# Moving w_out, g and graw by 64 bytes modulo 256 in SBUF, relative to x and w_in

## The chip, the cores and the metric

The kernel runs on one core of a Trainium2 chip. Its time is the device time of one execution in microseconds, from which a median of three runs is taken. A profile belongs to one further execution, with its own time.

## What is computed

18 blocks of 256 tokens go through an attention within chunks of 64 tokens, and then through a feed-forward layer with a rational function between its two products:

```
scores = scale * q_c @ k_c^T;  attn = softmax(scores);  x = attn @ v_c      # per chunk of 64, per head
h = x @ w_in                                   # (4608, 512) @ (512, 2048)
P = a0 + a1*h + a2*h^2 + a3*h^3
Q = 1 + |b0|*|h| + |b1|*h^2
g = P / (Q + 1e-6)
out = g @ w_out                                # (4608, 2048) @ (2048, 512)
```

## The kernel before

Each of x, w_in, g and w_out is split into a high part (F32R, a copy that keeps the upper bits) and a low part (the rest), and a product is the sum of high by high, high by low and low by high. Four kinds of work stand on TensorE:

- **ff1** (`ff1`, L340 to L352): h of one step, that is 512 of the 2048 hidden columns of one block. A call makes two of four groups of 12 matmuls 128x128 by 128x256; the weights that are loaded come from `wi_hi` or `wi_lo`, the moving operand from `xhi` or `xlo`. The result goes to the PSUM tile `ph`. A step has 48 matmuls, mostly in one run.
- **Second product in the early part** (`ff2`, L407 to L431): 48 matmuls for a step. Here g is loaded as weights (`ghi`, `glo`) and `wo` moves. Each pair covers the 512 columns of `wo` in two pieces of 256; at two places the cut is moved: by `CUT_FIRST` (24 columns) behind the small attention matmuls, and by `CUT_LAST` (48 columns: 304 and then 208) where an ff1 run comes next.
- **Second product in the fast part** (`fast_raw`, `fast_sum`, L624 to L643, all recorded at L619): from the seventh block on, a step takes 42 matmuls by a scheme with seven products for eight. The weights come from `graw` (18 matmuls) and from `shi` and `slo` (24), which lie in the buffers tagged `ghi` and `glo`; `wo` moves. There is no shifted cut here.
- **Attention**: 64 small matmuls (`quarters`, L225) for scores and for values, 8 transposes (L304).

The order is written out by hand: `START` for the first six blocks, `STEADY` for every later block. In `STEADY` a block has four ff1 runs; behind each stands the second product of an earlier step, and in three of the four the attention matmuls of a later block stand inside it: values behind 18 matmuls, scores behind 12, transposes behind 18. So the uninterrupted runs of the second product are 18 and 24, 12 and 30, 42, and again 18 and 24.

VectorE, ScalarE and GpSimd compute the rational function between the two products. SyncE's queue refetches parts of `wo` from DRAM (`fetch`, L601 to L604), since the scheme needs sums of blocks of w_out that replace some of its columns.

**Where the tiles lie.** Tiles lie behind each other in each partition's row of SBUF in the order in which they are first made. Their start addresses modulo 256 bytes, in the program as built, are: `wi_hi` and `wi_lo` 128, `xhi` and `xlo` 64, `wo` 128, the `ghi` and `glo` buffers 64, `graw` 64 (its buffer starts at 192, and 96 unused columns of 4 bytes stand ahead of it: 192 + 384 = 576). The slices that one matmul reads start at multiples of 512 bytes behind these, but for the shifted cuts. So while a weight load runs beside the matmul ahead of it, their operands start 64 bytes apart in one direction within ff1 (weights 128, moving 64), 64 bytes apart in the other direction within the second product (weights 64, moving 128), and at the same place modulo 256 where the one kind follows the other: the first weights of g (64) beside the last x (64), and the first weights of w_in (128) beside the last `wo` (128).

Of the kernel before, what the change touches and what calls it, by code (L numbers as in the profile page):

```python
# [10 lines left out]
F32 = mybir.dt.float32  # L11
F32R = mybir.dt.float32r
# [6 lines left out]
P = 128  # L19
# [56 lines left out]
def tile_chunked_attention_rational_moe(  # L76
# [12 lines left out]
    cp = ctx.enter_context(tc.tile_pool(name="cp", bufs=1))  # L89
    p2 = ctx.enter_context(tc.tile_pool(name="p2", bufs=2))  # L90
# [6 lines left out]

    wi_hi = cp.tile([P, NHP, DFF], F32R, tag="wi_hi", name="wi_hi")
    wi_lo = cp.tile([P, NHP, DFF], F32R, tag="wi_lo", name="wi_lo")
    wo = cp.tile([P, 2, 16, DM], F32R, tag="wo", name="wo")  # L100
    wo_hi, wo_lo = wo[:, 0], wo[:, 1]
    ident = cp.tile([P, P], F32, tag="ident", name="ident")
# [235 lines left out]
    ch, gbuf, obuf, accs = {}, {}, {}, {}  # L338
# [46 lines left out]

    def chain_ghi(n, s):
        h, A, B, C = ch[n, s]
        gbuf[n, s] = [p2.tile([P, FPS, BT], F32R, tag="ghi", name=f"ghi{n}_{s}"), None]
        nc.vector.scalar_tensor_tensor(gbuf[n, s][0], C, a0, A, ALU.add, ALU.mult)  # L389

# [39 lines left out]
                )  # L430
        before[0] = "ff2"  # L431

    co = p2.tile([P, 128], F32, tag="co", name="co", bufs=1)
    na0, na1, na2, na3, c0, kq, lsc, ebias, ib, b1m, nib = (co[:, i:i + 1] for i in range(11))

    def newton_reciprocal(_):
# [15 lines left out]
    def fast(g):  # L452
        return NST * FAST <= g < total - 2

    sbuf, graw = {}, {}
# [44 lines left out]
    def quads(x):  # L500
        return x.rearrange("p (j k) (i t) -> p j (k i) t", k=2, i=2)

    def new_hr(g):
        key = steps[g]
        C = ch[key][3]
        if not fast(g):
            gbuf[key] = [p2.tile([P, FPS, BT], F32R, tag="ghi", name=f"ghi{g}"), None]
            nc.scalar.copy(gbuf[key][0], C)
            return
        if g % 2 not in graw:  # L510
            t = p2.tile([P, 96 + 1536], F32R, tag="raw", name=f"graw{g % 2}", bufs=3)
            graw[g % 2] = t[:, 96:].rearrange("p (h j q t) -> p h j q t", h=2, j=2, q=3)
        nc.scalar.copy(graw[g % 2][:, 0], quads(C)[:, :, 1:4, :])  # L513

    def new_lr(g):
# [278 lines left out]
    for letter, f in zip("abcQIJpPgHRG", (  # L794
        chain_a, chain_b, chain_c, chain_q, chain_ln, chain_exp,
        chain_p, chain_p2, chain_ghi, chain_r1, chain_r2, chain_glo,
    )):
        do[letter] = of_step(f)
    do["Gp"] = lambda g: chain_glo(*steps[g], nc.gpsimd)
    for name, f in (  # L800
        ("ua", new_u), ("uc", new_c), ("uQ", new_v), ("uI", new_ln), ("uJ", new_exp), ("up", new_p), ("uP", new_p2),
        ("ug", new_t), ("uH", new_inv), ("uR", new_g), ("ue", new_hr), ("uGp", new_ls),
        ("uG", lambda g: new_ls(g, nc.vector)),
    ):
        do[name] = f

    def run(program, then=""):
# [11 lines left out]
    chain = {  # L819
        "U": new_u, "C": new_c, "V": new_v, "p": new_p, "p2": new_p2, "Ln": new_ln, "Ex": new_exp, "t": new_t,  # L820
        "A2": new_inv, "g": new_g, "hR": new_hr, "lR": new_lr, "s1": new_s1, "s2": new_s2, "s4": new_s4,
        "hS": new_hs, "lS": new_ls,
    }
# [81 lines left out]
    for b in range(FAST, NB + 1):  # L905
# [5 lines left out]
        for op, stage, shift in order:  # L911
# [3 lines left out]
            if stage is not None:  # L915
                g = NST * n + int(stage)
# [45 lines left out]
```

## Time and profile before

| | us |
|---|---|
| median of three runs | 872.11 (872.03 to 872.94) |
| the profiled execution | 870.93 |
| its span, first to last instruction | 869.1 |
| TensorE busy | 835.3 (96%) |
| VectorE busy | 741.9 (85%) |
| ScalarE busy | 539.1 (62%) |
| GpSimd busy | 523.5 (60%) |

The profiled execution is 1.2 us under the median, and 1.8 us of it lie outside the span. Matmuls are pipelined, so a matmul's own duration (some 279 ns) says little; the distance from the start of one to the start of the next, its pitch, is what adds up. Counts in the view of stretches include the matmuls that reach over a stretch's borders, so for the number in a run the code's count is taken.

### The profile page before, as it was taken

The page shows a single profiled execution, that of the slowest core. Times are in us where ns is not written, and L with a number is a line of the kernel's source. Part 1 is how long each engine was busy: PE and PEld are TensorE (multiplying, and loading weights), DVE is VectorE, ACT ScalarE, POOL GpSimd, SP SyncE. Part 2 cuts the span into 40 slices and gives each one's busy share as a digit, 9 for nine tenths or more (in the row PEclk, how much of TensorE's full clock was granted, in tenths as well). Part 3 has the DMA queues.
Part 4 walks back from the last instruction along what each step waited for, and adds up shares of the span by engine and source line. Part 5 has one row for each costly group of instructions (what it writes and reads, how often), then busy time and mean ns, then how long its engine had stood idle before and what let it go on. Part 6 is the DMA issues. An engine that isn't in the chain of part 4 may idle for free.

```text
span 869.1 us, 20986 instructions
## 1 busy us (share of the span) xinstructions
PE 835.3 (96%) x9084; PEld 825.7 (95%) x9084; DVE 741.9 (85%) x644; ACT 539.1 (62%) x541; POOL 523.5 (60%) x325
## 2 busy tenths in 40 slices
PE   2799989999999999999999999999999999999997
PEld 2799989999999999999999999999999999999996
DVE  5999997888778887888888888888888888898785
ACT  5998856466474656565666566666665665565652
POOL 1223234602877096776777777777787767686761
PEclk9999999999999999999999999999999999999999
DMA  8644433103132355767777786767676867766761
GB/s 317 252 174 155 146 123 91 32 2 99 49 122 74 133 193 163 237 216 227 243 239 245 220 253 205 253 214 251 210 252 221 254 219 248 236 220 203 257 212 33
DMA packets 125468, 162.85 MB, mean 187 GB/s; under 512 B 6848, under 2 KB 111296, under 8 KB 122304
## 3 DMA queue, kind: packets, MB, share of 16 engines
q1 hardware_dynamic: 125216, 161.25, 56.8%
q8 instruction: 71, 1.16, 0.6%
q10 hardware_dynamic: 160, 0.26, 0.1%
q14 instruction: 21, 0.17, 0.1%
HBM read 142.61 MB, written 18.87 MB: 186 GB/s over the span
## 4 chain that ended last, share of the span: by engine, by line
PE 86%; DVE 6%; DMA 4%; ACT 2%; issue 2%; SPq 1%; DVEq 0%; ACTq 0%
PE ph L352 41%; PE acc L619 14%; PE po L428 13%; PE acd L619 11%; DMA wo<-t 2%; PE psx L225 2%; PE pss L225 2%; PE pst L304 2%; DVE B L368 1%; DMA Bqk<-in_kT 1%; DMA raw<-in_w_out 1%; DMA out<-o 1%; DVE raw L186 1%; DVE B L393 0%; DVE C L380 0%
## 5 line engine op out<-in xcount | busy, mean ns | idle before, releaser
L352 PE MATMUL ph<-xhi,wi_hi 128*128 128x256 f32 x1152 | 321.6, 279 | 0.2 <-ACT at L308 0.2
L352 PE MATMUL ph<-xlo,wi_hi 128*128 128x256 f32 x1152 | 320.2, 278 | 0.8 <-DVE xlo L335 0.8
L352 PE MATMUL ph<-xhi,wi_lo 128*128 128x256 f32 x1152 | 319.9, 278 | 0.0
L352 PEld LDWEIGHTS ph<-xhi,wi_hi 128*128 128x128 f32 x1152 | 217.3, 189 | 0.9 <-ACT at L308 0.4
L352 PEld LDWEIGHTS ph<-xlo,wi_hi 128*128 128x128 f32 x1152 | 216.5, 188 | 1.3 <-DVE xlo L335 1.3
L352 PEld LDWEIGHTS ph<-xhi,wi_lo 128*128 128x128 f32 x1152 | 216.6, 188 | 0.0
L460 ACT ACTIVATE U<-ph 128x1024 f32<-128x1024 f32 x57 | 58.6, 1029 | 156.5 <-PE ph L352 156.1
L550 POOL TENSOR_TENSOR slo<-B,shi 128x1024 fp32r<-128x1024 f32 x46 | 110.7, 2407 | 69.7 <-ACT shi L542 67.5
L469 DVE SCALAR_TENSOR_TENSOR U<-U,co 128x1024 f32<-128x1024 f32 x57 | 98.2, 1724 | 23.9 <-ACT U L460 22.7
L490 DVE SCALAR_TENSOR_TENSOR U<-U,co,ph 128x1024 f32<-128x1024 f32 x57 | 71.9, 1262 | 44.4 <-ACT ph L486 44.1
L526 POOL TENSOR_TENSOR B<-C 128x512 f32<-128x512 f32 x46 | 68.7, 1494 | 54.6 <-DVE C L498 49.1
L428 PE MATMUL po<-wo,ghi 128*128 128x256 f32 (+3 forms) x768 | 94.0, 279 | 0.0
L428 PEld LDWEIGHTS po<-wo,ghi 128*128 128x128 f32 x768 | 91.0, 189 | 0.4 <-DVE ghi L389 0.2
L518 POOL TENSOR_TENSOR graw<-C,graw 128x768 fp32r<-128x768 f32 x46 | 85.5, 1859 | 0.7 <-ACT graw L513 0.7
L482 ACT ACTIVATE B<-U,cst,co 128x1024 f32<-128x1024 f32 x57 | 70.8, 1245 | 17.2 <-DVE U L469 16.8
L619 PE MATMUL acc<-wo,graw 128*128 128x256 f32 x552 | 79.4, 279 | 0.0
L486 ACT ACTIVATE ph<-B,co 128x1024 f32<-128x1024 f32 x57 | 63.9, 1120 | 17.5 <-DVE C L477 17.3
L498 DVE SCALAR_TENSOR_TENSOR C<-C,co,ph 128x1024 f32<-128x1024 f32 x57 | 73.0, 1281 | 2.0
L477 DVE SCALAR_TENSOR_TENSOR C<-C,co,ph 128x1024 f32<-128x1024 f32 x57 | 72.8, 1277 | 1.4
L494 DVE SCALAR_TENSOR_TENSOR ph<-U,ph 128x1024 f32<-128x1024 f32 x57 | 69.9, 1226 | 1.5
L619 PEld LDWEIGHTS acc<-wo,graw 128*128 128x128 f32 x552 | 70.0, 188 | 0.7
L473 DVE TENSOR_TENSOR C<-C,ph 128x1024 f32<-128x1024 f32 x57 | 69.0, 1210 | 1.8 <-ACT C L465 1.7
(105 smaller groups left out, 1630.1 us busy)
## 6 DMA issues: line engine op xcount, KB each, us to landing
wo<-t SPq DMA_DIRECT2D x90, 768.0 KB, 6.7
wo<-t SPq DMA_DIRECT2D x98, 256.0 KB, 3.3
out<-o SPq DMA_DIRECT2D x68, 128.0 KB, 6.3
raw<-in_w_out SPq DMA_DIRECT2D x8, 1024.0 KB, 5.1
raw<-in_w_in SPq DMA_DIRECT2D x8, 1024.0 KB, 5.1
v<-in_vP SPq DMA_DIRECT2D x20, 256.0 KB, 7.4
qk<-in_qT SPq DMA_DIRECT2D x36, 128.0 KB, 6.8
qk<-in_kT SPq DMA_DIRECT2D x36, 128.0 KB, 6.6
```

The costliest lines, as they stand in the source:

```text
L352: nc.tensor.matmul(ph[:, fi, :], w[:, cc, f], x[:, cc, :], start=(k == 0), stop=(k == len(mm) - 1))
L428: nc.tensor.matmul(accs[n][i][:, cols], g[:, fi, i * 128:(i + 1) * 128], w[:, FPS * s + fi, cols], start=start, stop=stop,)
L469: nc.vector.scalar_tensor_tensor(U, U, c0, U, ALU.add, ALU.mult)
L473: nc.vector.tensor_mul(C, C, h)
L477: nc.vector.scalar_tensor_tensor(C, C, na1, h, ALU.add, ALU.mult)
L482: nc.scalar.activation(ch[key][2], ch[key][1], AF.Ln, bias=cst[:, 0:1], scale=lsc)
L490: nc.vector.scalar_tensor_tensor(V, V, kq, h, ALU.add, ALU.mult)
L494: nc.vector.scalar_tensor_tensor(h, V, 2.0, h, ALU.subtract, ALU.mult)
L498: nc.vector.scalar_tensor_tensor(C, C, na0, h, ALU.add, ALU.mult)
L518: nc.gpsimd.tensor_sub(lo, quads(ch[steps[g]][3])[:, :, 1:4, :], hi.bitcast(F32))
L550: nc.gpsimd.tensor_sub(lo, sbuf[g], hi.bitcast(F32))
L619: nc.tensor.matmul(acc[n][pair][:, bank, col:col + 256], stat, mov, start=start, stop=stop)
```

## The change

Three tiles get other padding. 16 columns of 4 bytes ahead of `wo` move it by 64 bytes; 16 columns ahead of the first `ghi` buffer move `ghi` and `glo`; the padding inside `graw`'s buffer becomes 48 columns. The tile `co`, of which 11 columns are used, shrinks from 128 to 48 columns, by 320 bytes, so that with the 64 ahead of `wo` all between moves by a multiple of 256. Every instruction stays where it was on its engine, with the same operands and shapes; only addresses differ.

After it the starts modulo 256 are: `wi` 128 and x 64 as before; `wo` 192; `ghi`, `glo` and `graw` 128. Within ff1 and within the second product the distances between weights and moving operand are the same as before. Where the one kind follows the other they are now those of the kind that ends: g's weights (128) beside the last x (64), as w_in's weights stood beside x; w_in's weights (128) beside the last `wo` (192), as g's stood beside `wo`. At a cut shifted by 48 columns the last piece of `wo` starts 192 bytes further, before at 64, now at 128. `ident`, `nident`, `ab` and `cst` move by 64 bytes too; the attention's and the chain's tiles keep their places modulo 256.

```diff
@@ -97,6 +97,7 @@
     wi_hi = cp.tile([P, NHP, DFF], F32R, tag="wi_hi", name="wi_hi")
     wi_lo = cp.tile([P, NHP, DFF], F32R, tag="wi_lo", name="wi_lo")
+    cp.tile([P, 16], F32, tag="gap", name="wo_gap")
     wo = cp.tile([P, 2, 16, DM], F32R, tag="wo", name="wo")
@@ -385,6 +386,8 @@
     def chain_ghi(n, s):
         h, A, B, C = ch[n, s]
+        if not gbuf:
+            p2.tile([P, 16], F32, tag="gap", name="gap", bufs=1)
         gbuf[n, s] = [p2.tile([P, FPS, BT], F32R, tag="ghi", name=f"ghi{n}_{s}"), None]
@@ -430,7 +433,7 @@
-    co = p2.tile([P, 128], F32, tag="co", name="co", bufs=1)
+    co = p2.tile([P, 48], F32, tag="co", name="co", bufs=1)
@@ -508,8 +511,8 @@
-            t = p2.tile([P, 96 + 1536], F32R, tag="raw", name=f"graw{g % 2}", bufs=3)
-            graw[g % 2] = t[:, 96:].rearrange("p (h j q t) -> p h j q t", h=2, j=2, q=3)
+            t = p2.tile([P, 48 + 1536], F32R, tag="raw", name=f"graw{g % 2}", bufs=3)
+            graw[g % 2] = t[:, 48:].rearrange("p (h j q t) -> p h j q t", h=2, j=2, q=3)
```

## Rows read from the trace of the kernel before

**Rows 1.** The page: the span, and busy time by engine.
```profile
span 869.1 us, 20986 instructions
PE 835.3 (96%) x9084; PEld 825.7 (95%) x9084; DVE 741.9 (85%) x644; ACT 539.1 (62%) x541; POOL 523.5 (60%) x325
```
**Rows 2.** The page: the chain that ended last, by engine.
```profile
PE 86%; DVE 6%; DMA 4%; ACT 2%; issue 2%; SPq 1%; DVEq 0%; ACTq 0%
```
**Rows 3.** TensorE in order of time, a second product and ff1: start, us, operation, count.
```profile
413.66 0.39 PE L619 MATMUL acd<-wo,slo 128*128 128x256 f32 x2
413.89 0.39 PE L619 MATMUL acc<-wo,slo 128*128 128x256 f32 x2
414.11 0.28 PE L352 MATMUL ph<-xhi,wi_hi 128*128 128x256 f32 x1
414.23 0.28 PE L352 MATMUL ph<-xlo,wi_hi 128*128 128x256 f32 x1
414.35 0.28 PE L352 MATMUL ph<-xhi,wi_lo 128*128 128x256 f32 x1
```
**Rows 4.** The weight load beside the first of these ff1 matmuls.
```profile
414.12 0.19 PEld L352 LDWEIGHTS ph<-xlo,wi_hi 128*128 128x128 f32 x1
```
**Rows 5.** TensorE in order of time, an earlier place of the same kind.
```profile
392.03 0.40 PE L619 MATMUL acc<-wo,slo 128*128 128x256 f32 x2
392.27 0.28 PE L352 MATMUL ph<-xhi,wi_hi 128*128 128x256 f32 x1
392.39 0.28 PE L352 MATMUL ph<-xlo,wi_hi 128*128 128x256 f32 x1
392.50 0.28 PE L352 MATMUL ph<-xhi,wi_lo 128*128 128x256 f32 x1
392.62 0.28 PE L352 MATMUL ph<-xhi,wi_hi 128*128 128x256 f32 x1
392.73 0.28 PE L352 MATMUL ph<-xlo,wi_hi 128*128 128x256 f32 x1
```
**Rows 6.** Stretches, each one run: us, TensorE busy (instructions), clock, DMA share, GB/s.
```profile
409.35:414.11 4.76, 4.76 (x44) 1.00 0.66 211
414.11:419.77 5.66, 5.66 (x50) 1.00 0.92 293
419.77:421.90 2.13, 2.13 (x21) 1.00 0.85 274
422.69:425.60 2.91, 2.91 (x28) 1.00 0.76 191
425.60:431.05 5.45, 5.45 (x50) 1.00 0.95 305
509.71:511.76 2.05, 2.05 (x21) 1.00 0.93 315
808.25:813.90 5.65, 5.65 (x50) 1.00 0.99 320
813.90:818.85 4.95, 4.95 (x44) 1.00 0.71 257
270.03:275.69 5.66, 5.66 (x50) 1.00 0.00 0
275.69:277.58 1.89, 1.89 (x18) 1.00 0.00 0
```
**Rows 7.** Stretches of the early part: ff1 (120), ff1 (72), second product (96).
```profile
57.91:72.05 14.14, 14.14 (x123) 1.00 0.52 187
172.51:180.71 8.20, 8.20 (x74) 1.00 0.01 2
180.71:191.60 10.89, 10.89 (x99) 1.00 0.00 1
```
**Rows 8.** Groups by form: the pieces of 304 columns at shifted cuts.
```profile
L428 PE MATMUL po<-wo,ghi 128*128 128x304 f32 x13 | 3.9, 300 | 0.0
L428 PE MATMUL po<-wo,glo 128*128 128x304 f32 x8 | 2.4, 300 | 0.0
```
**Rows 9.** TensorE's waits for a refetched part of w_out: us, times, longest.
```profile
PE acd L619 <- DMA wo<-t: 1.1, 2, 0.7
```

## The prediction

> **What bounds the kernel now.** I read the busy times first: TensorE is busy for 835.3 of 869.1 us, the next engine for 741.9 [rows 1]. The chain of waits is TensorE for 86% [rows 2]. So what counts is how closely matmuls follow each other, and next I read TensorE in order of time, at places where one kind of product follows the other. There the reader is to see two pitches for one and the same form of matmul. In the second product that ends at 414.11, matmuls start 0.225 us apart by pairs, some 113 ns each; from 414.11 on, in ff1, they start 118 ns apart [rows 3]. At 392.03 it is the other way round: the second product runs at 0.24 us for two, some 118 ns each, and ff1 falls to 0.113 within three matmuls (392.27, 392.39, 392.50, 392.62, 392.73) [rows 5]. The weight load for the next matmul starts some 10 ns behind the start of the one ahead (414.12 and 414.11) [rows 3, 4], so both operands are read from SBUF side by side.
>
> The view of stretches then shows that a pitch holds for a whole run: ff1's 48 matmuls take 5.66 us behind the quick second product and 5.45 behind a slow one, at the same granted clock of 1.00 and with the DMAs as busy (0.92 and 0.95) [rows 6]. Per matmul that is 117.9 and 113.5 ns. It holds without any DMA too: 5.66 at 270.03, with the DMA share at 0.00 [rows 6]. So neither the clock nor a transfer makes the pitch. Neither does the kind of product: the 42 matmuls at 409.35 take 4.76 (113.3 ns), those at 813.90 take 4.95 (117.9 ns) [rows 6].
>
> I went through all 45 ff1 runs behind 341 us in this way. 31 stand behind a slow second product and turn quick as at 392.27; 3 stand behind one that an interruption had made slow, and are quick too. 9 stand behind an uninterrupted quick run of 42, and every one of them is slow, as at 414.11. 2 stand behind a slow one and stay slow (at 515.46 and 786.14). The second product behind an ff1 run keeps its pitch: the 18 matmuls take 2.13 behind the slow one and 2.05 behind a quick one [rows 6]. After the attention's matmuls it starts slow whatever was before (24 matmuls in 2.91) [rows 6].
>
> **The change part by part.** No instruction is added, removed or moved; the one effect is on addresses. The two pitches hang, by my theory, on how the stream of weights and the stream of moving columns meet modulo 256 bytes. Within ff1 and within the second product the operands are 64 bytes apart, and the quick pitch holds over whole runs there; only where the one kind follows the other do they start at the same place, and at exactly that place the pitch changes in 43 of the 45 cases. After the change that coincidence is gone: the pairs at these places are 64 bytes apart in the way that their own kind already has. A quick second product should then hand its pitch on to ff1, as ff1 does to the second product now.
>
> - The nine slow ff1 runs of the fast part: 5.66 less 5.45 is 0.21 each, 1.9 us [rows 6]. No row has a pitch under 113.3 ns, so 48 times that, 5.44, is the floor, and the term can't be over 9 times 0.22.
> - Behind seven of them stand 18 matmuls: 2.13 less 2.05, 0.08 each, 0.55 us. Behind the other two stand 42: 4.95 less 4.76, 0.19 each, 0.4 us [rows 6].
> - In the early part the ff1 run at 270.03 is of the same kind: 5.66 less 5.45, and the 16 matmuls behind it take 1.89 where 16 times 113.3 ns are 1.81: together 0.29 us [rows 6].
>
> The sum is 1.9 + 0.55 + 0.4 + 0.29, 3.1 us.
>
> What I cost at nothing, with its bounds. First, the turn from slow to quick at the 34 quick runs: at 392.27 three matmuls take 0.35 where 0.34 would do [rows 5]; if the turn gets smooth, 34 times 0.01, 0.35 us are gained, and if it fails, that is a rival below. Second, the 21 shifted cuts in the early part [rows 8]: their last piece stood at 64 beside w_in's weights and now stands at 128, the same place as they. I take none, since the piece is another length and the weight load there meets it at another time; the bounds are a loss of 4.0 us (below) and a gain of 1 us, 21 times some 0.05 for the uneven pitches around a cut. Third, the two slow runs at 515.46 and 786.14: they may turn quick, 0.6 us at the rates above, or stay. Fourth, the other engines' work on g, and the refetch of w_out into moved rows: TensorE waits for a transfer into `wo` for 1.1 us, two times, over the whole span [rows 9], and for no other engine between 340 and 700 us. That cover, TensorE being last everywhere, would be gone only if a block of 44.9 us got shorter by much more than the 0.3 us at stake; VectorE is busy for 85% [rows 1]. I bound it by the 3.1 us themselves on one side, and by 1.1 us of waits that could go on the other.
>
> One page speaks against the change. The Trainium skill, "SBUF — State Buffer", section "Who interferes with whom", gives TensorE two independent read ports, one for the moving operand and one for the weight load, and says that TensorE waits on no one. By that rule the two streams couldn't disturb each other, an address couldn't matter, and the sum would be 0. The rows don't settle it: the two pitches at one clock and one shape are something that the rule has no place for, but no row of this kernel varies an address alone.
>
> **The rivals.** *No change* (872.1): the pitch is set by when a weight load starts relative to the matmul ahead, whatever the addresses, and 414.11 comes out slow because ff1 follows the second product. For it: the interruptions change the pitch too, and those move no address. Against it: a quick ff1 run hands its pitch on, a quick second product never does, with instructions of the same shapes; so something about the operands decides.
>
> *The slow pitch is carried over* (slower): today 31 + 3 runs of ff1 turn quick behind a slow second product, and perhaps it is the coincidence at the boundary that shakes them out of the slow pitch. Without it, slow stays slow. For it: the turn happens at exactly the place whose addresses change, and ff1 can run slow for very long, 120 matmuls in 14.14 us at 57.91 [rows 7]. Against it: ff1 runs that start after attention matmuls, with no boundary of this kind, are found quick as well as slow. Its price: 34 times 0.21 for ff1, 7.1 us, and 72 matmuls of the second product per block (12, 42 and 18) at 4.5 ns more, 0.32 us in each of 11 blocks, 3.6 us: together 10.7 us, 882.8. It decides from the point where about 10 of the 34 runs stay slow, since one with what stands behind it costs 0.3 us against the 3.1 us gained.
>
> *The shifted cuts lose* (about 873): the cut of 48 columns puts `wo` at 64 before and at 128 now, so the coincidence is moved into the early part. By the order some 890 matmuls stand between such a cut and the next attention matmuls at the quick pitch now, as the 168 from 172.51 to 191.60, 19.09 us, 113.6 ns each [rows 7]. At 4.5 ns more each that is 4.0 us; with the 3.1 us gained the kernel ends 0.9 us slower at full price, unchanged at half.
>
> *More is gained* (867 and less): the early cuts, the two odd runs and the turns all get smooth as well, 2 us more; or the slow start after attention goes too, which is 24 or 30 matmuls at 4.5 ns for 34 runs, 4 us. Nothing in the addresses touches the latter, so I don't count on it.
>
> **How the numbers follow.** The sum is against the profiled execution: 870.9 less 3.1 is 867.8. That execution is 1.2 us under the median, and against the median of 872.1 the forecast is 869.0. I give the forecast a chance of 0.49, more gain 0.09, no change 0.17, the cuts 0.10, and the slow pitch carried over 0.15. About 0.2%, 1.7 us, is what a measurement of this kernel can tell from no change. Faster: 0.49 + 0.09 = 0.58. Same: 0.17, and 0.06 of the cuts, 0.23. Slower: 0.15 and 0.04, 0.19. The range goes from 866.5, which leaves out the larger half of "more is gained", to 873.5, which holds no change and the cuts at full price and leaves out the carried slow pitch: some 0.19 are outside. The forecast's own range is 867.5 to 870.2.
>
> **What would show it.** In the profile of the changed kernel the ff1 run behind each uninterrupted 42 should take 5.45 instead of 5.66 and the 18 behind it 2.05 instead of 2.13; the ff1 runs behind 24 and 30 should stay at 5.45. The early part's runs behind shifted cuts should still show 113 ns. The prediction is wrong if the run behind 42 is slow as before (then no change), if runs behind 24 and 30 take 5.66 (then the pitch is carried), or if the early part is longer by microseconds (then the cuts).

## The result, and the profile after

The changed kernel takes 881.75 us (median of 4 runs, 880.39 to 882.86), the kernel before 872.42 in the same comparison: a ratio of 1.0116, 95% interval [1.0097, 1.0135]. It is slower by 9.3 us; the forecast was 869.0, with a range up to 873.5. The profiled execution took 881.66.

The page gives the span, and busy times by engine, as [rows 1] do for the kernel before:

```profile
span 879.9 us, 20986 instructions
...
PE 847.8 (96%) x9084; PEld 839.0 (95%) x9084; DVE 736.3 (84%) x644; ACT 537.1 (61%) x541; POOL 523.8 (60%) x325
```

The span grew by 10.8 us and TensorE's busy time by 12.5, with as many instructions as before; the other engines' busy times stayed or fell. So it is not a longer wait on another engine that makes up the loss: TensorE's own matmuls follow each other more slowly. The stretches of TensorE have the columns of [rows 6]: us, busy and instructions, granted clock, DMA share, GB/s. The first is a second product of 96 matmuls of the early part, the last the 72 of ff1 ahead of it; the others are runs of two blocks of the fast part.

```profile
181.95:193.26 11.31, 11.31 (x98) 1.00 0.00 1
441.95:447.60 5.65, 5.65 (x50) 1.00 0.88 284
453.84:459.49 5.65, 5.65 (x51) 1.00 0.93 304
459.49:464.44 4.95, 4.95 (x45) 1.00 0.49 159
464.44:470.09 5.65, 5.65 (x51) 1.00 0.97 302
470.09:472.21 2.12, 2.12 (x20) 1.00 0.91 296
473.00:475.91 2.91, 2.91 (x27) 1.00 0.70 196
475.91:481.36 5.45, 5.45 (x50) 1.00 0.86 279
173.76:181.95 8.19, 8.19 (x74) 1.00 0.01 2
```

The reader is to see three things. Three of four ff1 runs take 5.65 now, where 5.45 was the rule (34 of 45 in the fast part); only the one behind the 24 matmuls that follow the transposes is quick (475.91). The 42 at 459.49 take 4.95 where those at 409.35 took 4.76 [rows 6]. And in the early part the 72 of ff1 are as quick as before (8.19, before 8.20), yet the 96 behind them take 11.31 where they took 10.89 [rows 7]: a quick ff1 run no longer hands its pitch on. The clock is 1.00 in every row.

In order of time (start, us, operation, count), the place that answers to [rows 5] shows no turn any more. The second product comes at 0.23 to 0.24 for two, and ff1 goes on at 0.12 after its first matmul:

```profile
441.71 0.40 PE L622 MATMUL acc<-wo,slo 128*128 128x256 f32 x2
441.95 0.28 PE L353 MATMUL ph<-xhi,wi_hi 128*128 128x256 f32 x1
442.06 0.28 PE L353 MATMUL ph<-xlo,wi_hi 128*128 128x256 f32 x1
442.18 0.28 PE L353 MATMUL ph<-xhi,wi_lo 128*128 128x256 f32 x1
442.30 0.28 PE L353 MATMUL ph<-xhi,wi_hi 128*128 128x256 f32 x1
```

**Where the time came from.** I took every run of matmuls of both traces, from its first start to the start of what follows, and added up the differences: +4.7 us for the second product of the early part, +4.6 for ff1 in the fast part, +3.5 for the second product there, and -2.0 for all else (waits at the start and around the attention's matmuls, ff1 in the early part). Counting pitches gives the same: 3620 pitches between matmuls lay between 112 and 114 ns before, 1150 now, and 2470 times 4.5 ns is 11.1 us. Of the 45 ff1 runs in the fast part, 10 are quick instead of 34: the ten behind the transposes' 24.

### The profile page after: what moved, and what is told of

The parts are those of the page before. It is cut to its first block, busy times and chain, and to the rows that moved or that the text cites. A ratio compares the mean times of both kernels' runs of the same rounds, so it can differ in the third digit from the quotient of the medians.

```text
span 879.9 us, 20986 instructions
## 1 busy us (share of the span) xinstructions
PE 847.8 (96%) x9084; PEld 839.0 (95%) x9084; DVE 736.3 (84%) x644; ACT 537.1 (61%) x541; POOL 523.8 (60%) x325
## 4 chain that ended last, share of the span: by engine, by line
PE 88%; DVE 5%; DMA 4%; issue 1%; ACT 1%; SPq 1%; DVEq 0%; ACTq 0%
PE ph L353 42%; PE acc L622 15%; PE po L431 14%; PE acd L622 11%; PE psx L226 2%; PE pss L226 2%; PE pst L305 2%; DMA wo<-t 1%; DVE raw L187 1%; DMA raw<-in_w_in 1%; DMA Bqk<-in_kT 1%; DMA out<-o 1%; DMA v<-in_vP 1%; DVE B L369 1%; DVE sm L289 0%
## 5 line engine op out<-in xcount | busy, mean ns | idle before, releaser
L353 PEld LDWEIGHTS ph<-xhi,wi_lo 128*128 128x128 f32 x1152 | 219.3, 190 | 0.0
L472 DVE SCALAR_TENSOR_TENSOR U<-U,co 128x1024 f32<-128x1024 f32 x57 | 91.9, 1614 | 33.5 <-ACT U L463 32.3
L431 PE MATMUL po<-wo,ghi 128*128 128x256 f32 (+3 forms) x768 | 98.1, 286 | 0.0
L431 PEld LDWEIGHTS po<-wo,ghi 128*128 128x128 f32 x768 | 95.1, 193 | 0.3
```

The lines of the kernel that those rows point to most:

```text
L353: nc.tensor.matmul(ph[:, fi, :], w[:, cc, f], x[:, cc, :], start=(k == 0), stop=(k == len(mm) - 1))
L431: nc.tensor.matmul(accs[n][i][:, cols], g[:, fi, i * 128:(i + 1) * 128], w[:, FPS * s + fi, cols], start=start, stop=stop,)
L472: nc.vector.scalar_tensor_tensor(U, U, c0, U, ALU.add, ALU.mult)
```

## The experiments

Every edit is one of padding, against the changed kernel, unless it says otherwise. To tell them apart I use the distance "weights minus moving", modulo 256 bytes, of the pair that TensorE reads side by side. Within ff1 it is +64 in all of them. The columns: this distance within the second product (Z), at the border from ff1 to it, at the border from it to ff1, the quick ff1 runs of the fast part in the profiled execution, and the median time.

| kernel | in Z | ff1 to Z | Z to ff1 | quick of 45 | us | ratio to before |
|---|---|---|---|---|---|---|
| before | -64 | 0 | 0 | 34 | 872.4 | 1 |
| after | -64 | +64 | -64 | 10 | 881.75 | 1.0116 [1.0097, 1.0135] |
| e1_wo | 128 | 0 | -64 | 21 | 883.89 | 1.0155 [1.0122, 1.0188] |
| e2_g | 0 | +64 | 0 | 45 | 878.68 | 1.0089 [1.0071, 1.0106] |
| e3_m64 | -64 | -64 | +64 | 37 | 868.95 | 0.9973 [0.996, 0.9987] |
| e4_128 | -64 | 128 | 128 | 11 | 879.29 | 1.0099 [1.0081, 1.0116] |
| e5_all | -64 | 0 | 0 | 32 | 871.71 | 1.0007 [0.9992, 1.0022] |
| e6_uni | +64 | +64 | +64 | 22 | 871.35 | 1.0001 [0.9983, 1.0018] |
| e12_border | -64 | +64 | 0 | 45 | 876.92 | 1.0073 [1.0059, 1.0087] |

The kernel before took 870.7 to 871.6 us in the comparisons of the experiments, so ratios are compared, not times. The number of quick runs differs from execution to execution too: 37 in e3_m64's profile, 35 in the repeat of the same kernel (e11_m64_again), 34 and 32 in the kernel before and e5_all. e6_uni's 22 belong to an execution of 874.01 us, 2.7 above its median.

**One half of the change each: w_out alone (e1_wo), g and graw alone (e2_g).**

```diff
# e1_wo
-        if not gbuf:
-            p2.tile([P, 16], F32, tag="gap", name="gap", bufs=1)
...
-            t = p2.tile([P, 48 + 1536], F32R, tag="raw", name=f"graw{g % 2}", bufs=3)
+            t = p2.tile([P, 96 + 1536], F32R, tag="raw", name=f"graw{g % 2}", bufs=3)
# e2_g
-    cp.tile([P, 16], F32, tag="gap", name="wo_gap")
...
-    co = p2.tile([P, 48], F32, tag="co", name="co", bufs=1)
+    co = p2.tile([P, 128], F32, tag="co", name="co", bufs=1)
```

> Only w_out's tile is moved by 64 bytes; g and graw lie as before. Boundary theory (what counts is the distance modulo 256 between weights and moving operand where one kind of product follows the other: 0 lets the second product stay quick behind a quick ff1 run, and 0 turns ff1 quick behind a slow second product): from ff1 to the second product the distance is 0 as before, from the second product to ff1 64 as in the changed kernel, so ff1 stays slow behind the slow 24 and 30 matmuls (5.65 us) and all behind it is slow: some 881 us, with the second product quick only where an ff1 run is quick. Own-place theory (what counts is where w_out or g lies, whatever lies beside it): one of the two moves makes the whole loss, so this is 872 or 882. The distance within the second product becomes 128, which no run has shown; the boundary theory takes it as no worse than 64.

> Only g and graw are moved by 64 bytes; w_out lies as before. Boundary theory: from the second product to ff1 the distance is 0 as before, so ff1 turns quick everywhere behind a slow second product (5.45 us); from ff1 to the second product it is 64 as in the changed kernel, so the second product is slow everywhere, behind quick ff1 runs too (18 matmuls in 2.12). Against the kernel before, 11 slow ff1 runs gain 0.2 us each, 2.3 us, and 72 matmuls of the second product per block lose 4.5 ns each in 11 blocks, 3.6 us: some 873.7 us. Own-place theory: 872 or 882, whichever the move of w_out alone is not. The distance within the second product becomes 0, which no run has shown over a whole run; if that alone is bad, the second product has a pitch above 118 ns and the time goes beyond 882.

Both are slower than before, so the loss does not belong to one tile's place: by the own-place theory one of the two would have been as quick as before. With g moved alone, the border from the second product to ff1 keeps its distance of 0, and all 45 ff1 runs turn quick behind second products that are slow. Stretches of e2_g, an ff1 run, 42 matmuls, an ff1 run:

```profile
453.57:459.03 5.46, 5.46 (x50) 1.00 0.90 298
459.03:464.05 5.02, 5.02 (x44) 1.00 0.61 199
464.05:469.51 5.46, 5.46 (x50) 1.00 0.90 283
```

The turn at this border was as expected; the time was 5 us above the expected 873.7, since the 42 in 5.02 are slower than any uninterrupted 42 of before (4.95 at most) and the early part's second product lost too (6.5 us): a distance of 0 within a product has a price of its own. With w_out moved alone the pitch within the second product is a mix of 115 to 123 ns (42 matmuls in 4.99), and half of the ff1 runs stay slow:

```profile
455.97:461.62 5.65, 5.65 (x50) 1.00 0.91 300
461.62:466.61 4.99, 4.99 (x45) 1.00 0.59 189
478.11:483.56 5.45, 5.45 (x50) 1.00 0.85 281
```

So neither half shows by itself what the whole change does: each also spoils the inside of the second product, which the whole change leaves alone.

**All tiles by 64 (e5_all).** If places matter by themselves, and not in relation to each other, this must change the time.

```diff
# e5_all, against the kernel before
+    cp.tile([P, 16], F32, tag="first", name="first_gap")
     wi_hi = cp.tile([P, NHP, DFF], F32R, tag="wi_hi", name="wi_hi")
```

> All tiles are moved by 64 bytes together, w_in and x and the attention's and the chain's too, so every distance is that of the kernel before and only the places themselves differ. Boundary theory: the time of the kernel before, 872.4 us, with ff1 at 5.45 behind 24 and 30 and 5.66 behind 42. Own-place theory: w_out at 192 and g at 128 are where the changed kernel has them, so 882 us.

Nothing changes (1.0007, with 1 inside the interval). What the changed kernel lost comes from the relations between tiles, not from their places.

**The same tiles the other way, by -64 (e3_m64, and again as e11_m64_again), and by 128 (e4_128).**

```diff
# e3_m64
-    cp.tile([P, 16], F32, tag="gap", name="wo_gap")
+    cp.tile([P, 48], F32, tag="gap", name="wo_gap")
...
-            p2.tile([P, 16], F32, tag="gap", name="gap", bufs=1)
+            p2.tile([P, 48], F32, tag="gap", name="gap", bufs=1)
...
-    co = p2.tile([P, 48], F32, tag="co", name="co", bufs=1)
+    co = p2.tile([P, 80], F32, tag="co", name="co", bufs=1)
...
-            t = p2.tile([P, 48 + 1536], F32R, tag="raw", name=f"graw{g % 2}", bufs=3)
+            t = p2.tile([P, 16 + 1536], F32R, tag="raw", name=f"graw{g % 2}", bufs=3)
# e4_128
-    cp.tile([P, 16], F32, tag="gap", name="wo_gap")
+    cp.tile([P, 32], F32, tag="gap", name="wo_gap")
...
-            p2.tile([P, 16], F32, tag="gap", name="gap", bufs=1)
+            p2.tile([P, 32], F32, tag="gap", name="gap", bufs=1)
...
-    co = p2.tile([P, 48], F32, tag="co", name="co", bufs=1)
+    co = p2.tile([P, 96], F32, tag="co", name="co", bufs=1)
...
-            t = p2.tile([P, 48 + 1536], F32R, tag="raw", name=f"graw{g % 2}", bufs=3)
+            t = p2.tile([P, 64 + 1536], F32R, tag="raw", name=f"graw{g % 2}", bufs=3)
```

> w_out, g and graw are all moved by 192 bytes (64 the other way): w_out at 64, g and graw at 0. Within each kind nothing changes; at the boundaries the pair now stands as the kind that begins has it, where in the changed kernel it stood as the kind that ends has it. Boundary theory: no distance of 0 is left, so slow stays slow and the second product is slow everywhere, as in the changed kernel: 882 us. Rival (it is the slip that a boundary pair makes in time, and its sign, that decides): the pitches come out another way than in both kernels, quick where the changed kernel is slow or the reverse, between 868 and 886. Own-place theory: not to be said from the two known points.

> w_out, g and graw all moved by 128 bytes: w_out at 0, g and graw at 192, the fourth of the four places in steps of 64. At both boundaries the pair stands 128 apart, which is neither 0 nor the distance of the kind that begins nor of the kind that ends. Theory of the kind that begins (a run is quick from its start if the pair at its border already has the run's own distance, as with 192 bytes): not given here, so the quick pitch is lost at borders, some 880 us, like the changed kernel. Theory of a sign (the weights' operand ahead of the moving one by less than half of 256 costs, behind it does not): 128 is the turning point and comes out between the two, 871 to 877 us.

> The kernel with wo, g and graw moved by 192 once more, unchanged, beside the kernel before and the two mixed versions on one chip. Theory: 869 us within 1.2, 0.25% under the kernel before. If the first result was chance: the same as before, 871 to 872.5.

My theory then was that the coincidence at the border is what turns slow into quick, so that any other distance is slow. e3_m64 refutes it: it is faster than the kernel before, twice (0.9973, and 0.9974 [0.9961, 0.9988] in the repeat). The theory that replaced it, that a run is quick from its start if the pair at its border has the run's own distance, had some 880 us for e4_128; it took 879.29 with 11 quick runs, where the theory of a sign had 871 to 877. Stretches of e3_m64: 30 matmuls, ff1, 42, ff1, 18, then the 24 behind the transposes, ff1:

```profile
442.94:446.58 3.64, 3.64 (x37) 1.00 0.38 102
446.58:452.02 5.44, 5.44 (x50) 1.00 0.92 301
452.02:456.78 4.76, 4.76 (x44) 1.00 0.59 191
456.78:462.22 5.44, 5.44 (x50) 1.00 0.95 308
462.22:464.27 2.05, 2.05 (x21) 1.00 0.99 319
465.06:467.97 2.91, 2.91 (x27) 1.00 0.67 189
467.97:473.63 5.66, 5.66 (x51) 1.00 0.98 304
```

Here is what the prediction hoped for: ff1 hands its quick pitch to the 42, and they hand it on to ff1. Between the profiles of e3_m64 and of the kernel before, the early part gained 2.7 us, ff1 in the fast part 1.0, and the second product there gave back 0.6, by waits of the kind that e12_border shows below. In this kernel the pair at a border has the distance of the kind that *begins*; in the changed kernel it has that of the kind that *ends*. In order of time, the turn from the slow 30 to ff1 is immediate:

```profile
446.35 0.40 PE L622 MATMUL acc<-wo,slo 128*128 128x256 f32 x2
446.58 0.28 PE L353 MATMUL ph<-xhi,wi_hi 128*128 128x256 f32 x1
446.69 0.28 PE L353 MATMUL ph<-xlo,wi_hi 128*128 128x256 f32 x1
```

**One distance everywhere (e6_uni), and without the shifted cuts (e7_uni_nocut, e8_m64_nocut).** If only a difference between distances disturbs, e6_uni should be the best of all.

```diff
# e6_uni
-    cp.tile([P, 16], F32, tag="gap", name="wo_gap")
+    cp.tile([P, 48], F32, tag="gap", name="wo_gap")
...
-    co = p2.tile([P, 48], F32, tag="co", name="co", bufs=1)
+    co = p2.tile([P, 80], F32, tag="co", name="co", bufs=1)
# e7_uni_nocut: e6_uni, and e8_m64_nocut: e3_m64, each with
-CUT_FIRST, CUT_LAST = 24, 48
+CUT_FIRST, CUT_LAST = 0, 0
```

> All weights at one place and all moving operands at another: w_in, g and graw at 128, x and w_out at 64. The second product then has ff1's distance, and so has every pair at a border. Theory of the kind that begins: quick handed over at every border, as with all moved by 192 bytes (869.0). Beyond that the second product starts again behind the attention's 64 small matmuls as ff1 does now, which is quick at once at 297 us: then 24 and 30 matmuls per block gain 4.5 ns each, 0.24 us in each of 11 blocks, 2.7 us, some 866.5 us; if it starts slow nevertheless but ff1 behind it is quick, 869; if the slow pitch is carried through ff1, up to 880.

> As the kernel with all weights at 128 and all moving operands at 64, and besides the shifted cuts of the early part are put back to 256 columns (24 and 48 become 0). Theory of the kind that begins: with no border that loses the quick pitch the shifted cuts are of no use, and each costs some 0.03 to 0.05 us of uneven pitches, 21 of them 0.6 to 1 us: that much quicker than with the cuts. Rival: the cuts still turn slow runs quick behind attention in the early part, and without them it is 1 to 3 us slower.

> As the kernel with w_out, g and graw moved by 192 bytes (869.0), with the shifted cuts of the early part put back to 256 columns. Theory of the kind that begins: 0.5 to 1 us quicker, since quick is handed over without them. Rival: the cuts turn slow runs quick behind the attention's matmuls (the second product starts slow there), and without them the slow pitch goes on through ff1 in the early part: 1 to 3 us slower.

It isn't. With equal distances a border changes nothing, in either direction: in the fast part 22 ff1 runs are quick behind a quick second product and 23 slow behind a slow one, and none differs from what stands ahead of it. Stretches of e6_uni: a quick ff1 run; 24 behind the transposes, slow, and the ff1 run behind them; 24 behind the matmuls for values:

```profile
447.67:453.11 5.44, 5.44 (x51) 1.00 0.95 301
466.35:469.26 2.91, 2.91 (x28) 1.00 0.62 185
469.26:474.91 5.65, 5.65 (x50) 1.00 0.90 280
478.21:481.04 2.83, 2.83 (x31) 1.00 0.68 193
```

A slow start stays slow until something interrupts the stream, and a quick one stays quick. The last row is new: at +64 the second product can be quick at once behind values (2.83; at -64 2.93, in all 11 blocks of the kernels before and after). Without cuts e6_uni loses half a per cent (876.65 us, 1.0056 [1.0031, 1.0081]): in the early part 363 instead of 975 pitches of ff1 are quick. So in that kernel the cuts are what takes the stream out of the slow pitch, as the rival had it, at a larger price than its 1 to 3 us. For e3_m64, whose borders do that themselves, the cuts hardly matter: 870.08 us, 0.9983 [0.9968, 0.9997] without them. Against 0.9973 [0.996, 0.9987] with them, that settles neither the small gain that the theory had nor the small loss of its rival.

**Mixed places (e9_mix, e10_mix2).** w_out at 64 as in e3_m64; graw at 0 and the other buffers of g at 128, or the other way round.

```diff
# e9_mix
-    cp.tile([P, 16], F32, tag="gap", name="wo_gap")
+    cp.tile([P, 48], F32, tag="gap", name="wo_gap")
...
-    co = p2.tile([P, 48], F32, tag="co", name="co", bufs=1)
+    co = p2.tile([P, 80], F32, tag="co", name="co", bufs=1)
...
-            t = p2.tile([P, 48 + 1536], F32R, tag="raw", name=f"graw{g % 2}", bufs=3)
+            t = p2.tile([P, 16 + 1536], F32R, tag="raw", name=f"graw{g % 2}", bufs=3)
# e10_mix2
-    cp.tile([P, 16], F32, tag="gap", name="wo_gap")
+    cp.tile([P, 48], F32, tag="gap", name="wo_gap")
...
-            p2.tile([P, 16], F32, tag="gap", name="gap", bufs=1)
+            p2.tile([P, 48], F32, tag="gap", name="gap", bufs=1)
...
-    co = p2.tile([P, 48], F32, tag="co", name="co", bufs=1)
+    co = p2.tile([P, 80], F32, tag="co", name="co", bufs=1)
```

> wo at 64, ghi, glo, shi and slo at 128, graw at 0 (x at 64, w_in at 128 as in all). Theory, that the distance of the pair at a border decides: where ff1 ends in front of graw's 18, the pair (0 beside 64) has the distance of the second product, as in the kernel with all three moved by 192; where the second product ends with slo (128) in front of ff1, the pair is w_in at 128 beside wo at 64. The early part's second product and the 24 of the fast part (shi, slo at 128, wo at 64) then have ff1's distance, as with equal distances everywhere, where the 24 behind the attention's matmuls were quick at once (2.83 us). It expects: ff1 quick in 37 or more of 45 runs, the 24 behind matmuls for scores and values in 2.73 to 2.83 us instead of 2.91, 42 in 4.76, and 866 to 867.5 us. Rival, that a run of the second product must keep one distance: the change from graw to shi inside an uninterrupted 42 costs the quick pitch, 42 in some 4.88, the ff1 run behind it 5.65 in 11 blocks: 871 or more.

> wo at 64, ghi, glo, shi and slo at 0, graw at 128. The other half of the mix: where ff1 ends in front of graw's 18 the pair is 128 beside x at 64, ff1's own distance, and graw stands beside wo at ff1's distance; the 24 and the early part are as in the kernel with all three moved by 192. Theory of the border pair: graw's 18 keep ff1's pitch as with equal distances (2.05 quick), the 24 behind the attention's matmuls start slow (2.91) and are quick from the next ff1 run on: 868 to 870. Rival, one distance for a whole run: the 42 lose the quick pitch at the 18th, and ff1 behind it is slow in 11 blocks: 872 or more.

The slice in front of `graw` (`t[:, 16:]` or `t[:, 48:]`) goes with its padding, as in the kernels above. They took 868.15 (0.9967 [0.9947, 0.9987]) and 869.42 us (0.9976 [0.9961, 0.9991]), where e3_m64's repeat beside them took 869.58. All three are faster than before; the intervals do not tell them apart. In e9_mix the 30 and the 24 behind the attention's matmuls got quick, as expected (3.53 and 2.84):

```profile
442.29:445.82 3.53, 3.53 (x37) 1.00 0.37 101
476.37:479.21 2.84, 2.84 (x31) 1.00 0.72 193
```

but only 4 of its 14 runs of 42 ahead of ff1 took 4.76, and 35 ff1 runs were quick, not 37 or more (a difference that e3_m64 and its repeat show too). In e10_mix2 38 were quick, so the change from graw to shi inside a run does not by itself cost the quick pitch. The gain at one place was given back at others, by slow starts that stick as in e6_uni and by interruptions: in e9_mix's trace, 9 of the 15 runs of 42 stop ahead of their first `shi` weights, with over 170 ns between two starts, for 2.8 us in all; in the kernel before 3 do, for 1.1. What they wait for is shown next.

**One operand at one border (e12_border).** The kernels so far move whole tiles, so each changes several distances. This one is the changed kernel, except that the last matmul of each run ahead of ff1 reads its 256 columns of w_out 16 columns earlier, at 128 modulo 256. That product then takes other columns than it should, so this kernel is one to learn from, not to use.

```diff
-            mov = wo[:, h, FPS * s + 2 * j + where[3], where[4]:where[4] + 256]
+            first = where[4] - (16 if last else 0)
+            mov = wo[:, h, FPS * s + 2 * j + where[3], first:first + 256]
...
+                        last=name == "3" and half == 1 and j == 1,
```

> The changed kernel, with one matmul altered in each run of the fast part's second product that stands ahead of ff1: the last one reads wo 16 columns earlier, from 128 modulo 256 instead of 192 (so that product takes other columns than the reference). All tiles, all other operands and the early part are those of the changed kernel. Theory, that the pair at the border alone decides: w_in's weights (128) now load beside a moving operand at 128, as in the kernel before, so ff1 turns quick behind the slow second product; of 45 ff1 runs 44 or 45 are quick instead of 10, the second product stays slow everywhere (42 in 4.95, 18 in 2.12 to 2.21), and 35 times 0.2 = 7 us are gone: 874.7, between 873.5 and 876. Rival, that the places of whole tiles decide, with the matmuls before the last setting how ff1 is entered: 10 of 45 quick as in the changed kernel, 881 to 882.

All 45 ff1 runs are quick, instead of 10, and the second product stays slow. In order of time, at the place shown for the changed kernel:

```profile
440.70 0.40 PE L623 MATMUL acc<-wo,slo 128*128 128x256 f32 x2
440.94 0.28 PE L353 MATMUL ph<-xhi,wi_hi 128*128 128x256 f32 x1
441.06 0.28 PE L353 MATMUL ph<-xlo,wi_hi 128*128 128x256 f32 x1
441.18 0.28 PE L353 MATMUL ph<-xhi,wi_lo 128*128 128x256 f32 x1
441.29 0.28 PE L353 MATMUL ph<-xhi,wi_hi 128*128 128x256 f32 x1
441.41 0.28 PE L353 MATMUL ph<-xlo,wi_hi 128*128 128x256 f32 x1
441.52 0.28 PE L353 MATMUL ph<-xhi,wi_lo 128*128 128x256 f32 x1
```

After three matmuls at 0.12 ff1 falls to 0.11, as in [rows 5]. So the address of this one operand decides, and not the places of whole tiles. The time is 876.92 us where 874.7 was expected: of the 7 us that were to be gained against the changed kernel, the two profiled spans show 5.1 (879.9 and 874.8), the ratios some 3.8. Stretches of the ff1 run behind the place just shown, and of a run of 42, the ff1 run behind it, and the 18:

```profile
440.94:446.39 5.45, 5.45 (x50) 1.00 0.90 289
458.09:463.35 5.26, 5.19 (x44) 1.00 0.62 200
463.35:468.81 5.46, 5.46 (x51) 1.00 0.84 265
468.81:470.93 2.12, 2.12 (x21) 1.00 0.93 313
```

The 42 at 458.09 take 5.26 instead of 4.95, with a stop ahead of the first matmul on `shi`, at 460.44. Four rows on it: the weight load's wait (for what, us in all, times, longest), ScalarE's copy of `shi` (ns, start), the issue of a refetch of part of w_out (start, us), and that transfer's time from issue to landing:

```profile
PEld acd L623 <- ACT C L468: 0.3, 1, 0.3
L545 ACT CAST shi<-B x1: 1037/1037/1037, 452.8 to 452.8; 128x1024 fp32r<-128x1024 f32 x1
452.59 0.36 SPq L607 DMA_DIRECT2D wo<-t  x1
DMA to landing us min/median/max: 7.7/7.7/7.7
```

The first row names an instruction of ScalarE, but the copy of `shi` had ended at 453.8. The refetched part landed at 460.31, and the wait on that queue ends 0.03 us behind it. The same holds at all five such stops of this trace, at e9_mix's nine and at the three of the kernel before: each ends 0.03 us behind the landing of such a refetch. This refetch is issued as the run ahead of ff1 ends (ff1 starts at 452.63), and at the stops it takes 7.4 us or more. ff1 and the 18 behind it cover 7.8 us of it at the slow pitch (5.65 and 2.12), 7.5 at the quick one (5.44 and 2.05). ff1 gains 6.6 us in the fast part against the changed kernel, and the 14 runs of 42 ahead of ff1 together give back 1.6: with a shorter block, the refetch of w_out comes last there.

## Why the prediction was wrong

- *What bounds the kernel, and what decides.* Right: TensorE's pitch sets the time; it moved with clock and instructions unchanged, by addresses alone. The rival of no change is refuted by the result. The rule of the Trainium skill weighed there ("SBUF — State Buffer", section "Who interferes with whom": two independent read ports for TensorE, and no waiting) would have given a change of 0. Measured were 9.3 us for the whole change, and 0.19 us per ff1 run for one operand's address in e12_border. The measurement decides: addresses of TensorE's own reads do change its pitch.
- *The step that failed* is "A quick second product should then hand its pitch on to ff1, as ff1 does to the second product now". I took any distance that one of the two kinds has by itself to be smooth at a border, and so took the border from ff1 to the second product, which worked, to go on working though the change moved it from 0 to +64. Before, the second product is quick behind each of the 50 quick ff1 runs ahead of it in both parts; after, it is slow behind each of the 22. In e3_m64 it is quick behind all 59, in e6_uni behind all 42. So the runs show a direction: with the distance of the kind that begins the quick pitch crosses both borders (e3_m64, e6_uni); with that of the kind that ends it is lost from ff1 to the second product, and the slow one is carried on to ff1 (after). So no 42 was quick any more, and the three terms of the sum (1.9, 0.55 and 0.4 us) had nothing to come from. The early term of 0.29 fell too: the 48 of ff1 that took 5.66 at 270.03 take 5.65 now.
- *The turn at the 34 quick ff1 runs*, costed at 0 with a rival behind it, was the main loss in ff1. The rival named the mechanism, "the slow pitch is carried over", with a chance of 0.15 and 882.8 us. Its price came out near, but by two errors that cancel: it took 7.1 us for ff1, where 4.6 were lost, because the ten runs behind the transposes' 24 are quick, two of which had been slow; and it left out the early part's second product, 4.7 us. So its size was luck, its mechanism was not. The 3.6 us for the second product in the fast part were 3.5.
- *The shifted cuts.* The cost of nothing holds at the cut itself: ff1 behind it is still quick (8.19 for 72). In the early part of the changed kernel all nine turns from slow to quick stand at one of the 16 borders with a cut shifted by 48, whose last piece lies at 128 as w_in's weights do, and none at the five borders without one: a distance of 0 again, in the same execution. The early part lost what that rival had priced (4.0 us) for another reason, the border from ff1 into the second product.
- *The two odd runs* at 515.46 and 786.14 turned quick (5.45 both), as allowed for. The waits for refetched parts of w_out are 1.1 us by the row of waits, as before [rows 9].
- *Two readings* were off, without weight for the sum: of the nine runs of 42 called uninterrupted, two had stopped for a refetch (4.91 at 454.29, 5.71 at 824.30) and were quick all the same; and 16 of the 21 shifted cuts stand directly ahead of ff1, so the bounds on them counted some that are no border.

Only argued, or open: why the distance of the kind that begins is the good one. It fits all kernels above, but from ff1 to the second product no run changed one operand alone, and which read is held up, and for how long, no view shows. Nor did w_in and x ever move against each other: at the border to ff1 no run tells w_out's distance to the first weights from its distance to the first x. That weights and moving columns are the partners is argued from e1_wo and e2_g, where within the second product only this distance changed, and the pitch with it. Steps of 64 bytes alone were tried; that only the remainder by 256 counts is assumed. Also open is why slow turns quick in e3_m64 behind scores and values but not behind the transposes' 24, and why those 24 alone still help ff1 in the changed kernel.

## What to carry to other kernels

When one form of matmul shows two pitches at one clock, look at where a run is entered: the operands read at the border can set the pitch for the whole run, so one wrong address is paid 48 times. Where two streams alternate, compute the distance from weights to moving columns modulo 256 for each border apart and in its direction, and try both signs of a shift: here +64 cost 1.2% and -64 gained 0.27%. Before counting a quicker pitch as time won, look at what comes last in the shortened block: here a transfer that the slow pitch had covered. And where a view names an engine that had long been done, look for the transfer that ended beside it.

## What the hardware showed that was not expected

- The address of one moving operand, the last before ff1, decides between 5.65 and 5.45 us for the 48 matmuls behind it (10 and 45 quick runs of 45); a shift of all tiles by 64 bytes does nothing (1.0007).
- Distances of 0 and 128 bytes between weights and moving columns, held over a whole run, are slower than the slow pitch at 64: 5.02 and 4.99 against 4.95 for 42 matmuls.
- At -64 a second product behind the attention's values started slow in every block (2.93 for 24, some 118 ns each), at +64 it could start quick (2.83).
- The refetch of part of w_out takes about as long as the matmuls that cover it (7.7 us against 7.6 in the block shown of e12_border). So a quicker TensorE meets it more often: 9 of 15 runs of 42 stop for it in e9_mix, 3 in the kernel before.
